# Layer one's blocks 2 and 3: both h stages first, then y by seven products, with the weight work placed anew

## The chip, the core and the metric

One core of a Trainium2 chip runs one program. Its engines are TensorE (PE), VectorE (DVE), ScalarE (ACT), GpSimd (POOL) and SyncE (SP), each with a queue of its own that is worked off in program order; all DMAs of this kernel are issued on SP. The metric is the device time in microseconds of one execution.

## What is computed

Local attention over 4 batches, 8 heads, 768 tokens (chunks of 32 queries with 16 keys to the left, 8 to the right and 8 memory keys), and then two feed-forward layers on the 3072 tokens of width 512, with an inner width of 2048, all in fp32:

```python
out[:, :, c_start:c_end] = np.matmul(a, v_full)      # a: softmax over 64 keys
...
h = x @ w_in                                         # layer one
g = np.maximum(h, 0.0) + np.log1p(np.exp(-np.abs(h)))
y = g @ w_out
...
h = y @ w_in2                                        # layer two
g = h - np.tanh(h)
return (g @ w_out2).astype(np.float32)
```

## The kernel before

**Precision.** Every fp32 operand is split into a high part (a cast, on ACT) and a low part (the difference, on DVE), and each product is three matmuls (`mm3`, L385): high by high, high by low, low by high. A matmul has 128 rows of weights and 512 columns.

**Blocks.** The tokens are six blocks of 512. Layer one's block 0 runs while weights arrive, in an order written out by hand (`OPENING`). Blocks 1, 2 and 3 are plain (L925): for each of 16 slices f of the inner width PE does h(f), 12 matmuls into one of two banks `ps_h`, then y(f-2), 12 matmuls into four banks `ps_y`; ACT takes the softplus of h(f) and casts it to `gh`, DVE subtracts for `gl`. The weights of layer one stay in 16 slots of SBUF, `w0` to `w15`, but two slices that share one slot are fetched again in each block (`load_w1`).

**Blocks in pairs.** Blocks 4 and 5 of layer one, and all three pairs of blocks of layer two, use a scheme with seven products in place of eight for a 2 by 2 product of halves (`PRODUCTS`). All h of the pair come first, g stays in SBUF (`g2`), and then `y_phase` (L740) runs seven products over eight pairs of slices p: 56 steps of six matmuls. For each step `y_steps` (L695) casts the operand to `gh` on ACT and subtracts for `gl` on DVE; the operand of step s+3 is prepared right behind step s (`AHEAD` = 3), and `gh` and `gl` have three buffers each. The summed weights of this scheme are made on the chip by jobs and kept in DRAM (`wod[0]` for layer one, `wid` and `wod[1]` for layer two); `Ring` loads them in halves of 1,024 KB, each of which serves four steps, into five slots. Results of a product are copied or added in `after_y`.

**Ticks.** `tick` (L783) is called all through these stages, some 322 times, about every 12 matmuls, and hands out all other work by number: `JOBS` says at which tick each job starts. `job_w1` sums layer one's weights, `job_w` converts, sums and splits one of layer two's 16 weight pieces (it loads raw data into a single slot, waits `LEAD` = 4 ticks, then starts on ACT), and `job_x` prepares layer one's output as layer two's input.

**Attention.** Units 8 to 23 (128 tokens each) start every six ticks in `ATT_ORDER`. At the unit's tick 0 PE computes its scores into `ps_a` and the value product of the unit before; DVE takes maximum and difference; at tick 1 ACT takes one exponential of 512 columns; at tick 2 DVE sums and normalises (four instructions); at tick 4 PE transposes and ACT copies. Softplus and exponential lie in different tables of ACT, so an ACT_TABLE_LOAD stands at each change. Units 20 to 22 belong to block 5, whose x tile is still in use by block 3, so they go through DRAM (`VIA_DRAM`, `x1d`).

Of the kernel before, what the change touches and what calls it, by code (L numbers as in the profile page):

```python
# [22 lines left out]
P = 128  # L23
# [15 lines left out]
ATT_STEP = 6  # L39
ATT_ORDER = (8, 9, 10, 11, 20, 12, 13, 14, 15, 21, 16, 17, 18, 19, 22, 23)  # L40
VIA_DRAM = (20, 21, 22)
# [34 lines left out]
PLAIN = NB - 2  # L76
# [4 lines left out]
GSLOT = (8, 9, 10, 11, 12, 13, 14, 7)  # L81
JOBS = (
    (1, 15, 24, 43, 53, 76, 85, 94),
    (5, 14, 23, 33, 66, 75, 84, 92, 95, 99, 102, 106, 109, 113, 117, 152),
    (42, 54, 159, 169, 214, 224),
)
SECOND = (95, 102, 109, 117)
PHASES = ((1, NT - 1),) + tuple((2, b) for b in range(NT))
# [8 lines left out]
def attention_ffn_ffn(  # L97
# [38 lines left out]
    x1d = dpool.tile([P, KT, 2, N], F32, name="x1d")  # L136
# [230 lines left out]
    def x_out(u):  # L367
        src = att.pop(u)["x"]
        o = (u % UB) * P
        if u in VIA_DRAM:  # L370
            x = opool.tile([P, KT, 2, P], F32R, name="o")
        else:
            x = x_tile(u // UB)[:, :, :, o : o + P]
# [71 lines left out]

    def split_to(src, dst, shape):
# [12 lines left out]
    def job_w(kind, p, second=False):  # L459
# [7 lines left out]
        c = pool.tile([P, 4 * HALF], U32, name=name, bufs=1)  # L467
        nc.scalar.mul(c.bitcast(F32), hi.bitcast(F32), EXP_BIAS)
        yield
        nc.vector.tensor_scalar(out=c, in0=c, scalar1=3, scalar2=None, op0=ALU.logical_shift_left)  # L470
        for of, k, op in ((hi, 0x80000000, ALU.bitwise_and), (lo, 29, ALU.logical_shift_right)):
            nc.vector.scalar_tensor_tensor(
                out=c, in0=of, scalar=k, in1=c, op0=op, op1=ALU.bitwise_or
            )
            yield
# [10 lines left out]
        yield from split_to(w, lambda s: ((0, 4, place(s, 2, 4)),), [4, HALF])  # L486

    def sums(w):
# [3 lines left out]
        nc.vector.tensor_tensor(out=w[:, 2], in0=w[:, 2], in1=w[:, 1], op=sub)  # L492
        nc.vector.tensor_tensor(out=w[:, 3], in0=w[:, 3], in1=w[:, 1], op=sub)  # L493
# [12 lines left out]
    def job_w1(p):  # L506
        c = tpool.tile([P, 4, HALF], F32, name="c2", bufs=1)
# [10 lines left out]
    def job_x(b, e, second=False):  # L518
        raw = wpool.tile([P, 2, 2, N], F32, name="w6" if second else "w15")
# [6 lines left out]
        def high(q, src):  # L526
            if b and q in (2, 5, 7):
# [62 lines left out]
    def half_of_y(b, q, p):  # L590
        return b, "y", q, p // (NP // 2)

    uses = [
        u
        for b, (layer, _) in enumerate(PHASES)
        for u in [half_of_h(b, p, i) for p, i in h_order if layer == 2]
        + [half_of_y(b, q, p) for q in PRODUCTS for p in range(NP)]
    ]
    last_use = {u: i for i, u in enumerate(uses)}

    class Ring:
        def __init__(self, slots):
            self.todo, self.at, self.used = list(dict.fromkeys(uses)), {}, 0
            for t in slots:
                self.add(t)
# [28 lines left out]
    def kept(ps):  # L634
        t = lpool.tile([P, N], F32, name="kept", bufs=4)
# [82 lines left out]
    def after_y(b, q, d, ps):  # L718
        for _ in range(d):
            yield  # L720
        if q in (1, 6, 5):
            held[d, q] = kept(ps)
# [17 lines left out]
    def y_phase(b, prep, prepared):  # L740
        for i, q in enumerate(PRODUCTS):
            ps = [banks[(2 * b + d) % 4][i % 2] for d in range(2)]
            for p in range(NP):
# [6 lines left out]
                if p == NP // 2 and b + 1 < len(PHASES):  # L750
# [32 lines left out]
    def tick(chain=iter(())):  # L783
# [5 lines left out]
        i, r = divmod(k, ATT_STEP)  # L789
        u = ATT_ORDER[i] if i < len(ATT_ORDER) else None  # L790
        before = ATT_ORDER[i - 1] if 0 < i <= len(ATT_ORDER) else None
        if u is not None:
            if r == 1:
                if i + 2 < len(ATT_ORDER):
                    qk_load(ATT_ORDER[i + 2])
                if 0 < i < len(ATT_ORDER) - 1:
                    v_load(ATT_ORDER[i + 1])
# [3 lines left out]
        if r == 1 and before in VIA_DRAM:  # L801
            run(soft.pop(("x", before)))
# [8 lines left out]
        if r == 4 and u is not None:  # L811
            t_mm(u, ps_a[:, 0, :])
        next(chain, None)
        if r == 4 and u is not None:
# [5 lines left out]
        if r == 0 and u is not None:  # L820
            soft[u] = softmax(u)
# [5 lines left out]
    with tc.manual_schedule(engines={mybir.EngineType.PE}):  # L827
# [91 lines left out]
        def t_load(u):  # L919
            t = wpool.tile([P, 2, 2, 512], F32R, name=f"w{u % T_RING}")  # L920
# [3 lines left out]

        for j in range(1, PLAIN):  # L925
            x = x_tile(j)
            for f in range(NF):
                ps = ff_h(f, ps_h[slot % 2], x)
                tick(chain1((1, j, f), ps, nc.scalar))
                pend.append((j, f))  # L930
                run_y()
                if f == SHARED[0] + LAG:
                    defer(load_w1, SHARED[1])
                elif f == LAG - 1 and j > 1:
                    defer(load_w1, SHARED[0])
                if j == PLAIN - 1 and 0 <= f - LAG < T_RING:
                    defer(t_load, f - LAG)
                tick()
                slot += 1

        xs = [x_tile(PLAIN), None]
        steps = []
        for f in range(NF + T_LAG):
            steps += [(0, f)] * (f < NF) + [(1, f - T_LAG)] * (f >= T_LAG)
        lpool = None

        def act_g(g, ps, g0):
            softplus(g, ps)
            yield
            if g0 is not None:  # L950
                minus(g, g, g0)

        for n, (t, f) in enumerate(steps):
            ps = ps_h[(slot + n) % 2] if n < 4 else (*ps_y, *ps_h)[(n - 4) % 6]
            weights["i", f] = w1t["i", f]
            ff_h(f, ps, xs[t])
# [3 lines left out]
            if n == len(steps) - 1:  # L960
                prepared = []
                prep = y_steps(prepared)
                for _ in range(AHEAD):
                    next(prep)
            tick(act_g(g, ps, g2[f][:, 0] if t and f < NP else None))
# [3 lines left out]
            if n == 0:  # L969
                xs[1] = x_tile(PLAIN + 1)  # L970
                nc.sync.dma_start(
                    out=xs[1].bitcast(F32).rearrange("p k s n -> p (k s) n")[:, :, : P * len(VIA_DRAM)],
                    in_=x1d.rearrange("p k s n -> p (k s) n")[:, :, : P * len(VIA_DRAM)],
                )
            if now[0] > AT_END + 1 and lpool is None:
# [6 lines left out]
                ring = Ring([lpool.tile([P, 2048], F32R, name="ring")])  # L982
            if t and f % 2 and f // 2 + T_RING < NP:
                defer(t_load, f // 2 + T_RING)
            elif f == NF - 1:
                for i in (0, 2048):
                    defer(ring.add, xs[t].rearrange("p k s n -> p (k s n)")[:, i : i + 2048])
        banks = [ps_b, tuple(ps_h), tuple(ps_y[:2]), tuple(ps_y[2:])]
        for b, (layer, _) in enumerate(PHASES):
            if layer == 2:  # L990
                prepared = []
                prep = y_steps(prepared)
                h_phase(b, prep)
# [70 lines left out]
```

## Time and profile before

| what | value |
|---|---|
| median of 3 runs | 1057.54 us (1057.13 to 1058.17) |
| the profiled execution | 1057.51 us, span 1055.4 us |
| PE busy | 1044.2 us, 99% |
| DVE, ACT busy | 727.6 us (69%), 567.1 us (54%) |
| DMA | 303.19 MB, mean 287 GB/s |

The span runs from the first to the last instruction; 2.1 us of the execution's time lie outside it. PE is busy nearly all the time, so time can go where PE gets less work, and come where PE has to wait.

### The profile page before, as it was taken

To read this page: it belongs to the slowest core of one execution; us is meant where nothing else is said; L and a number is where in the kernel's file an instruction comes from. 1 tells how busy PE (TensorE), PEld (TensorE's weight loads), DVE (VectorE), ACT (ScalarE), POOL (GpSimd) and SP (SyncE) were. 2 spreads that over 40 slices of the span, in tenths; PEclk is the share of its full clock that TensorE was granted. 3 is DMA by queue.
4 is the path that set the end of the run, shared out by engine and by line. 5 is a ranking of instruction groups with operands and counts; after the bars stand their busy time and mean duration, and the time that the engine had idled before them with its cause. 6 is when DMAs were issued, how large, how long until landed. Compare 5 with 4: busy or idle time off the path is not lost.

```text
span 1055.4 us, 18458 instructions
## 1 busy us (share of the span) xinstructions
PE 1044.2 (99%) x7368; PEld 857.4 (81%) x7370; DVE 727.6 (69%) x1129; ACT 567.1 (54%) x904; POOL 7.8 (1%) x14
## 2 busy tenths in 40 slices
PE   7999999999999999999999999999999999999998
PEld 5787888888888888888888888888888888888886
DVE  6998445845755657487677687777487877446876
ACT  6996454645656455354454555544455554344553
POOL 2000000000000000000000000000000000000000
PEclk8999999999999999999999999999999999999999
DMA  9989945857777986999987999978799788656651
GB/s 377 407 327 358 337 171 186 301 187 236 263 248 248 312 307 195 341 361 352 325 326 281 359 371 347 341 294 320 272 363 347 293 321 305 224 170 213 243 202 61
DMA packets 101269, 303.19 MB, mean 287 GB/s; under 512 B 8000, under 2 KB 55104, under 8 KB 83520
## 3 DMA queue, kind: packets, MB, share of 16 engines
q1 hardware_dynamic: 101184, 302.02, 79.5%
q8 instruction: 58, 0.95, 0.4%
q14 instruction: 27, 0.22, 0.1%
HBM read 211.29 MB, written 90.70 MB: 286 GB/s over the span
## 4 chain that ended last, share of the span: by engine, by line
PE 97%; DVE 1%; ACT 1%; DMA 0%; issue 0%; ACTq 0%
PE ps_y L387 47%; PE ps_h L387 32%; PE ps_b L387 13%; PE ps_a L361 2%; PE ps_a L280 1%; PE ps_a L332 1%; PE ps_h L880 1%; DMA qk<-in_qk 0%; PE ps_yy L361 0%; PE ps_h L399 0%; DVE gl L427 0%; DVE t L307 0%; DVE x L327 0%; ACT o L170 0%; PE ps_a L268 0%
## 5 line engine op out<-in xcount | busy, mean ns | idle before, releaser
L387 PE MATMUL ps_h<-x,w 128*128 128x512 f32 x900 | 215.3, 390 | 0.1
L704 ACT CAST gh<-w 128x512 fp32r<-128x512 f32 x224 | 139.0, 622 | 140.3 <-DVE gl L645 120.2
L645 DVE TENSOR_TENSOR gl<-w,gh 128x512 fp32r<-128x512 f32 x236 | 163.0, 691 | 71.4 <-ACT gh L704 64.9
L387 PEld LDWEIGHTS ps_h<-x,w 128*128 128x128 f32 x900 | 168.6, 188 | 35.4 <-ACT t L410 0.2
L387 PE MATMUL ps_y<-gh,w 128*128 128x512 f32 x512 | 172.9, 399 | 0.0
L387 PEld LDWEIGHTS ps_y<-gh,w 128*128 128x128 f32 x512 | 96.1, 188 | 21.3
L387 PE MATMUL ps_y<-gh,x 128*128 128x512 f32 x352 | 109.4, 389 | 0.0
L387 PE MATMUL ps_y<-gl,w 128*128 128x512 f32 x256 | 99.7, 390 | 0.0
L387 PE MATMUL ps_y<-w,x 128*128 128x512 f32 x402 | 94.5, 389 | 0.0
L387 PEld LDWEIGHTS ps_y<-w,x 128*128 128x128 f32 x402 | 75.5, 188 | 15.7
L427 DVE TENSOR_TENSOR gl<-t,gh 128x512 fp32r<-128x512 f32 x64 | 45.5, 713 | 55.8 <-ACT gh L422 55.6
L668 ACT ACTIVATE tanh<-sum 128x512 f32<-128x512 f32 x72 | 45.5, 632 | 60.0 <-DVE sum L641 59.8
L387 PEld LDWEIGHTS ps_y<-gh,x 128*128 128x128 f32 x352 | 66.1, 188 | 13.7
L410 ACT ACTIVATE t<-ps_h 128x512 f32<-128x512 f32 x64 | 38.1, 598 | 69.4 <-PE ps_h L387 65.8
L387 PE MATMUL ps_b<-gh,x 128*128 128x512 f32 x176 | 68.5, 389 | 0.0
L387 PE MATMUL ps_h<-gh,x 128*128 128x512 f32 x176 | 68.5, 389 | 0.0
L387 PE MATMUL ps_y<-gl,x 128*128 128x512 f32 x176 | 68.5, 389 | 0.0
L448 ACT CAST o<-c 128x1024 fp32r<-128x1024 f32 (+1 forms) x32 | 31.0, 969 | 69.6 <-DVE c L493 41.1
L645 DVE TENSOR_TENSOR w<-w 128x512 f32<-128x512 f32 x88 | 60.5, 688 | 6.8 <-ACT w L410 5.8
L387 PEld LDWEIGHTS ps_y<-gl,w 128*128 128x128 f32 x256 | 48.2, 188 | 9.0
L387 PE MATMUL ps_y<-x,w 128*128 128x512 f32 x240 | 55.2, 389 | 0.0
L387 PE MATMUL ps_b<-w,x 128*128 128x512 f32 x216 | 54.8, 389 | 0.0
(160 smaller groups left out, 1611.6 us busy)
## 6 DMA issues: line engine op xcount, KB each, us to landing
x<-wod SPq DMA_DIRECT2D x44, 1024.0 KB, 4.7
w<-x2d SPq DMA_DIRECT2D x21, 1024.0 KB, 6.8
x<-wid SPq DMA_DIRECT2D x21, 1024.0 KB, 6.1
wod<-o SPq DMA_DIRECT2D x32, 512.0 KB, 6.1
qk<-in_qk SPq DMA_DIRECT2D x21, 768.0 KB, 6.5
x2d<-o SPq DMA_DIRECT2D x30, 512.0 KB, 7.2
x<-wid SPq DMA_DIRECT2D x18, 768.0 KB, 6.8
ring<-wod SPq DMA_DIRECT2D x12, 1024.0 KB, 5.3
```

What stands on the lines that cost most here:

```text
L280: nc.tensor.matmul(out=ps[cc, j, KEYS * p : KEYS * (p + 1)], lhsT=a["q"][r, p, cc], rhs=a["k"][r, c, p, :], start=True, stop=True,)
L332: nc.tensor.transpose(ps[:, p * P : (p + 1) * P], a["sm"][:, p * P : (p + 1) * P], ident)
L361: nc.tensor.matmul(out=ps[h : h + 64, p % 2, 2 * P + t0 : 2 * P + t0 + CHUNK], lhsT=v, rhs=pT, start=True, stop=True,)
L387: nc.tensor.matmul(out=ps, lhsT=a, rhs=b, start=first and i == 0, stop=last and i == 2, skip_group_check=on,)
L410: nc.scalar.activation(out=out, in_=x, func=AF.Softplus)
L427: eng.tensor_tensor(out=gl, in0=t, in1=gh.bitcast(F32), op=ALU.subtract)
L448: nc.scalar.copy(out=hi, in_=src)
L645: nc.vector.tensor_tensor(out=out, in0=x, in1=y, op=ALU.subtract)
L668: nc.scalar.activation(out=t, in_=h, func=AF.Tanh)
L704: nc.scalar.copy(out=gh, in_=src)
L880: nc.tensor.matmul(out=ps_h[1], lhsT=zeros[:, :P], rhs=zeros, start=True, stop=True)
```

## The change

- Blocks 2 and 3 become a pair as well: 16 h steps of block 2, 16 of block 3 in reversed order, then `y_phase(0)`, which is 56 steps. Layer one's input weights for this come back from DRAM (`T1_LOADS`), the summed output weights through a ring in slots `w0` to `w4`.
- Attention units go in plain order at ticks `ATT_AT`; the x tiles are free by then, and the way through DRAM is gone. Units 20 to 23 now fall into the y stage of the new pair. Units 10, 11, 21 and 22 (`LATE_ACT`) take their softmax with eight exponentials of 64 columns on ACT, which also subtract and sum.
- All `job_w1` run in block 1. Of the 16 `job_w`, seven start before tick 56, eight from tick 89 to 131 and one at 148; none starts from tick 56 to 88. Nine of them (`BY_ACT`) do more of the conversion on ACT, in three activations of 1024 columns. `split_halves` splits in halves into `gh` and `gl` buffers between ticks 105 and 121.

```diff
-ATT_STEP = 6
-ATT_ORDER = (8, 9, 10, 11, 20, 12, 13, 14, 15, 21, 16, 17, 18, 19, 22, 23)
+ATT_AT = (0, 6, 14, 20, 28, 33, 38, 42, 46, 50, 54, 59, 64, 68, 74, 86, 92)
...
+    (8, 15, 27, 37, 43, 49, 55, 89, 96, 99, 102, 105, 108, 111, 131, 148, ),
+    (86, 94, 156, 169, 206, 220, ),
...
+BY_ACT = (8, 15, 27, 55, 99, 108, 111, 131, 148, )
+T1_LOADS = {9: 0, 13: 1, 17: 2, 21: 3, 25: 4, 29: 5, 33: 6, 38: 7, 54: 0}
+LATE_ACT = (10, 11, 21, 22, )
-PHASES = ((1, NT - 1),) + tuple((2, b) for b in range(NT))
+PHASES = ((1, 1), (1, 2)) + tuple((2, b) for b in range(NT))
...
+        if by_act:
+            x = pool.tile([P, 4 * HALF, 2], U16, name=name, bufs=1)
+            nc.scalar.mul(x[:, :, 1].bitcast(F16), hi.bitcast(F32), SIGN_ONLY)
+            nc.scalar.activation(
+                out=x[:, :, 0], in_=lo, func=AF.Identity, scale=LOW_SCALE, bias=low_bias
+            )
+            nc.scalar.mul(hi.bitcast(F32), hi.bitcast(F32), EXP_BIAS)
+            yield
...
+                if not b and p % 4 == 3 and i * 2 + p // 4 >= 9:
+                    s = i * 2 + p // 4 - 9
+                    defer(t_load, s, s)
...
-            soft[u] = softmax(u)
+            soft[u] = softmax(u, u in LATE_ACT)
...
-        for j in range(1, PLAIN):
...
+        steps = [(0, f) for f in range(NF)] + [(1, f) for f in reversed(range(NF))]
+        prepared = []
+        t2 = []
+        prep = y_steps(prepared, t2)
+        ring = Ring((0,), ())
+        for n, (t, f) in enumerate(steps):
+            if t and f == NP - 1:
+                t2.extend(t2_tiles())
+            h_step(n, n == len(steps) - 1, t, f, x_tile(2 + t), t and f < NP and t2)
             if pend:
                 run_y()
                 tick()
...
+            if t and f % 2 == 0 and f < 2 * T_RING:
+                s = T1_RING[T_RING - 1 - f // 2]
+                defer(lambda s=s: ring.add(wpool.tile([P, 2048], F32R, name=f"w{s}")))
+        y_phase(0, prep, prepared)
```

How the order of instructions moves, at three places. On PE, in the middle of block 3 before (`w_...` are weight slots, x the block's input):

```order
L387 MATMUL ps_h_82<-x_2793,w_1020 128x512 x12
L387 MATMUL ps_y_670<-gh,w_890 128x512
L387 MATMUL ps_y_670<-gl,w_890 128x512
L387 MATMUL ps_y_670<-gh,w_890 128x512
L387 MATMUL ps_y_671<-gh,w_890 128x512
L387 MATMUL ps_y_671<-gl,w_890 128x512
L387 MATMUL ps_y_671<-gh,w_890 128x512
```

and on PE in the y stage of blocks 2 and 3 now, where unit 20 hands over to unit 21 (L367 is the value product, L286 the scores):

```order
L367 MATMUL ps_a<-pT,v 64x32 x32
L286 MATMUL ps_a<-qk 32x64 x32
L384 MATMUL ps_y_669<-gh,w_3701 128x512
L384 MATMUL ps_y_669<-gl,w_3701 128x512
L384 MATMUL ps_y_669<-gh,w_3701 128x512
L384 MATMUL ps_y_671<-gh,w_3701 128x512
L384 MATMUL ps_y_671<-gl,w_3701 128x512
L384 MATMUL ps_y_671<-gh,w_3701 128x512
```

A pair `gh`, `gl` served twelve matmuls and an h of another twelve stood between; now each pair serves six, with no h between, and attention stands among them.

On ACT, at one unit's scores and exponential in a plain block before (L375 copies the unit before, `o<-c` is a weight job, t and gh are block 2's softplus):

```order
L375 CAST x_3794<-ps_a 128x2x2x128
L321 ACT_TABLE_LOAD
L321 ACTIVATE sm<-sm 128x512
L448 CAST o<-c_3882 128x768
L410 ACT_TABLE_LOAD
L410 ACTIVATE t<-ps_h_82 128x512
L422 CAST gh<-t 128x512
```

and at unit 21 in the y stage of blocks 2 and 3 now (each `gh<-w` prepares one step, `t<-ps_y` is the copy of product 1):

```order
L378 CAST x_4044<-ps_a 128x2x2x128
L748 CAST gh<-w_2727 128x512
L748 CAST gh<-w_2781 128x512
L677 COPY t<-ps_y_669 128x512
L322 ACT_TABLE_LOAD
L322 ACTIVATE sm,st<-ps_a,st 128x64 x8
L748 CAST gh<-w_2802 128x512
L677 COPY t<-ps_y_671 128x512
L748 CAST gh<-w_2825 128x512
```

The table load and the eight exponentials now stand between the casts of two neighbouring steps, those of steps 10 and 11.

On ACT, at the last weight job in layer one's last y stage before:

```order
L704 CAST gh<-w_4977 128x512
L704 CAST gh<-w_5018 128x512
L704 CAST gh<-w_5061 128x512
L468 ACTIVATE c_6088<-w_5998 128x1024
L726 COPY o<-ps_h_81 128x512
```

and at the last but one in the same stage now:

```order
L748 CAST gh<-w_5568 128x512 x3
L487 ACTIVATE c_5814<-w_5718 128x1024
L488 ACTIVATE c_5814<-w_5718,low_bias 128x1024
L491 ACTIVATE w_5718<-w_5718 128x1024
L748 CAST gh<-w_5568 128x512
L748 CAST gh<-w_4869 128x512
```

The one activation stood behind the stage's last cast; now three stand in its middle, between the casts of steps 22 and 23.

## Rows read from the trace of the kernel before

**Rows 1.** The page's first part: busy us, share and instructions of each engine.

```profile
PE 1044.2 (99%) x7368; PEld 857.4 (81%) x7370; DVE 727.6 (69%) x1129; ACT 567.1 (54%) x904; POOL 7.8 (1%) x14
```

**Rows 2.** Stretches: block 1, block 3, blocks 4/5 h, blocks 4/5 y.

```profile
core 0: us, PE busy (x) PEld busy (x) DVE busy (x) ACT busy (x) POOL busy (x), PEclk, DMA share, GB/s
123.10:223.50 100.40, 100.40 (x1107) 82.38 (x1106) 58.74 (x100) 53.10 (x71) 0.00 (x0) 1.00 0.60 209
...
324.00:424.50 100.50, 100.50 (x1050) 82.68 (x1050) 62.69 (x109) 53.88 (x73) 0.00 (x0) 1.00 0.75 263
424.50:518.30 93.80, 93.80 (x474) 77.53 (x473) 62.73 (x87) 42.53 (x62) 0.00 (x0) 1.00 0.96 338
518.30:594.40 76.10, 76.10 (x337) 63.03 (x336) 55.42 (x85) 37.54 (x61) 0.00 (x0) 1.00 0.88 333
```

**Rows 3.** The chain that ended last: start us, us, what.

```profile
378.20 2.72 PE ps_y L387 x12
...
442.27 10.88 PE ps_y L387 x48
```

**Rows 4.** PE's timeline: start us, us, instruction, idle before and releaser.

```profile
105.10 0.63 PE L332 MATMUL ps_a<-ident,sm 128*128 128x128 f32 x4 [1.23 <-DVE sm L327]
...
143.76 1.14 PE L361 MATMUL ps_a<-pT,v 64*64 64x32 f32 x64
144.82 0.86 PE L280 MATMUL ps_a<-qk 64*32 64x64 f32 x64
```

**Rows 5.** ACT's timeline in layer one's last y stage.

```profile
533.43 0.62 ACT L704 CAST gh<-w 128x512 fp32r<-128x512 f32 x1 [0.74 <-DVE gl L645]
534.79 0.62 ACT L704 CAST gh<-w 128x512 fp32r<-128x512 f32 x1 [0.74 <-DVE gl L645]
```

**Rows 6.** DVE's timeline, at a unit's normalisation and in that y stage.

```profile
103.11 0.69 DVE L324 TENSOR_REDUCE st<-sm 128x8 f32<-128x512 f32 x1 [2.08 <-ACT sm L321]
...
104.27 0.69 DVE L327 TENSOR_TENSOR sm<-sm,st 128x512 f32<-128x512 f32 x1
...
534.08 0.69 DVE L645 TENSOR_TENSOR gl<-w,gh 128x512 fp32r<-128x512 f32 x1 [0.67 <-ACT gh L704]
```

**Rows 7.** ACT's timeline in the opening, at unit 5's eight exponentials.

```profile
84.33 1.28 ACT L316 ACT_TABLE_LOAD   x1
85.63 0.31 ACT L316 ACTIVATE sm<-ps_a,st 128x64 f32<-128x64 f32 x1
...
87.86 0.24 ACT L316 ACTIVATION_READ_ACCUMULATOR sm<-ps_a,st 128x1 f32 x1
```

**Rows 8.** Groups by line and shape: xcount, busy us, mean ns, idle before.

```profile
L472 DVE SCALAR_TENSOR_TENSOR c<-w,c 128x1024 uint32<-128x1024 uint32 x24 | 29.4, 1223 | 0.6
...
L468 ACT ACTIVATE c<-w 128x1024 f32<-128x1024 f32 x12 | 13.6, 1133 | 5.1 <-DVE o L452 5.1
...
L174 ACT ACTIVATE c<-w,low_bias 128x1024 uint16<-128x1024 uint32 x4 | 5.9, 1469 | 0.0
L173 ACT ACTIVATE c<-w 128x1024 f16<-128x1024 f32 x4 | 5.5, 1384 | 0.0
```

**Rows 9.** Stretches of the opening, columns as in rows 2.

```profile
15.00:20.00 5.00, 2.68 (x74) 2.12 (x75) 4.71 (x13) 5.00 (x25) 0.00 (x0) 1.00 1.03 408
20.00:25.00 5.00, 4.91 (x176) 4.58 (x178) 4.58 (x9) 4.32 (x8) 1.66 (x1) 0.58 1.03 410
...
104.00:106.00 2.00, 0.90 (x6) 0.88 (x7) 0.89 (x2) 0.23 (x1) 0.00 (x0) 1.00 1.00 355
```

**Rows 10.** DMA issues by line: xcount, KB each, median us from issue to landing.

```profile
x<-wod SPq DMA_DIRECT2D x44, 1024.0 KB, 4.7
...
w<-w1id SPq DMA_DIRECT2D x8, 1024.0 KB, 8.4
w<-in_w2o SPq DMA_DIRECT2D x8, 1024.0 KB, 8.4
```

**Rows 11.** SP's timeline: layer one's last input weights, issued in the last h stage.

```profile
479.15 0.46 SPq L921 DMA_DIRECT2D w<-w1id  x1
```

More of the change, by code (lines that the diff above doesn't have):

```diff
@@ L1 @@
+from bisect import bisect_right
 from contextlib import ExitStack
@@ L444, in out1, with split_halves @@
             defer(nc.sync.dma_start, y1d[j // 2][e % 2][:, j % 2, e // 2], o, more=1)
+    def split_halves(src, dst):
+        for s in range(2):
+            ts = []
+            for i in (0, 2):
+                t = gpool.tile([P, 2, HALF], F32R, name="gl" if s else "gh")
+                if s:
+                    nc.vector.tensor_tensor(
+                        out=t, in0=src[:, i : i + 2], in1=his[i // 2].bitcast(F32), op=ALU.subtract
+                    )
+                else:
+                    nc.scalar.copy(out=t, in_=src[:, i : i + 2])
+                ts.append(t)
+            if s:
+                for i, t in enumerate(ts):
+                    defer(put, t, ((0, 2, dst(1, 2 * i)),))
+            else:
+                his = ts
+                yield
+                for i, t in enumerate(ts):
+                    put(t, ((0, 2, dst(0, 2 * i)),))
     def split_to(src, dst, shape):
@@ L457, in put, with job_w @@
             nc.sync.dma_start(out=place, in_=t[:, at : at + n].bitcast(F32))
-    def job_w(kind, p, second=False):
+    def job_w(kind, p, second=False, by_act=False):
         src = w2i if kind == "i" else w2o
@@ L485, in job_w @@
         yield
-        yield from split_to(w, lambda s: ((0, 4, place(s, 2, 4)),), [4, HALF])
+        if T2_H[0] <= now[0] < T2_H[1]:
+            yield from split_halves(w, lambda s, i: place(s, 2 + i, 2))
+        else:
+            yield from split_to(w, lambda s: ((0, 4, place(s, 2, 4)),), [4, HALF])
     def sums(w):
@@ L591, in half_of_y, with __init__ @@
         return b, "y", q, p // (NP // 2)
[L593 to L599, printed above, removed]
-    class Ring:
-        def __init__(self, slots):
-            self.todo, self.at, self.used = list(dict.fromkeys(uses)), {}, 0
+    class Ring:
+        def __init__(self, phases, slots):
+            self.uses = [
+                u
+                for b in phases
+                for u in [half_of_h(b, p, i) for p, i in h_order if PHASES[b][0] == 2]
+                + [half_of_y(b, q, p) for q in PRODUCTS for p in range(NP)]
+            ]
+            self.last_use = {u: i for i, u in enumerate(self.uses)}
+            self.todo, self.at, self.used = list(dict.fromkeys(self.uses)), {}, 0
             for t in slots:
@@ L721, in after_y @@
         if q in (1, 6, 5):
[L722 removed]
+            held[d, q] = kept(ps, d, q)
             return
@@ L741, in y_phase @@
         for i, q in enumerate(PRODUCTS):
-            ps = [banks[(2 * b + d) % 4][i % 2] for d in range(2)]
+            ps = [(banks[2 * (b - 1) + d & 3] if b else ps_y[2 * d : 2 * d + 2])[i % 2] for d in range(2)]
             for p in range(NP):
@@ L800, in tick @@
                 run(soft.pop(u))
-        if r == 1 and before in VIA_DRAM:
-            run(soft.pop(("x", before)))
+        if k in T1_LOADS:
+            t_load(T1_LOADS[k], T1_SLOT[T1_LOADS[k]])
         active.extend(job() for job in plan.get(k, ()))
@@ L923, in t_load, with act_g @@
                 w1t["i", 2 * u + i] = t[:, i, 0], t[:, i, 1]
-        for j in range(1, PLAIN):
[L926 to L944, printed above, removed]
-        lpool = None
-        def act_g(g, ps, g0):
+        lpool = None
+        x = x_tile(1)
+        for f in range(NF):
+            ps = ff_h(f, ps_h[slot % 2], x)
+            tick(chain1((1, 1, f), ps, nc.scalar))
+            pend.append((1, f))
+            run_y()
+            if f == SHARED[0] + LAG:
+                defer(load_w1, SHARED[1])
+            tick()
+            slot += 1
+        def act_g(g, ps, g0, f=0, t2=None):
             softplus(g, ps)
@@ L959, in attention_ffn_ffn @@
             g = g2[f % NP][:, 2 * (f // NP) + t]
-            if n == len(steps) - 1:
-                prepared = []
-                prep = y_steps(prepared)
+            if last:
                 for _ in range(AHEAD):
                     next(prep)
-            tick(act_g(g, ps, g2[f][:, 0] if t and f < NP else None))
+            step()
+            tick(act_g(g, ps, g2[f][:, 0] if t and f < NP else None, f, t2))
+        steps = [(0, f) for f in range(NF)] + [(1, f) for f in reversed(range(NF))]
[7 more added lines that the diff above has]
+            h_step(n, n == len(steps) - 1, t, f, x_tile(2 + t), t and f < NP and t2)
             if pend:
@@ L968, in attention_ffn_ffn @@
                 tick()
[L969 to L975, printed above, removed]
+            if t and f % 2 == 0 and f < 2 * T_RING:
+                s = T1_RING[T_RING - 1 - f // 2]
+                defer(lambda s=s: ring.add(wpool.tile([P, 2048], F32R, name=f"w{s}")))
+        y_phase(0, prep, prepared)
+        steps = []
+        for f in range(NF + T_LAG):
+            steps += [(0, f)] * (f < NF) + [(1, f - T_LAG)] * (f >= T_LAG)
+        prepared = []
+        prep = y_steps(prepared)
+        for n, (t, f) in enumerate(steps):
+            x = x_tile(2 * (NT - 1) + t)
+            h_step(n, n == len(steps) - 1, t, f, x)
+            if now[0] > ATT_AT[-1] + 1 and lpool is None:
                 attention.close()
```

146 lines of the change are left out of this document (79 added, 67 removed).

## The prediction

> **What bounds the kernel now.** I read the page's busy times first: PE is busy 1044.2 of 1055.4 us, DVE 727.6, ACT 567.1 [rows 1]. A mean can hide stages with another limit, so the table of stretches comes next: from 123 us on PE is busy for the whole of each stage, plain or paired, at the full granted clock, while DVE and ACT have a quarter to a half of each free [rows 2]. The chain that ended last says the same: twelve matmuls take 2.72 us in a plain block and forty-eight take 10.88 us in a paired one, 0.2267 us each in both [rows 3]. The last PE wait that I found is 1.23 us at 105 us, where transposes wait for a unit's normalisation [rows 4], before the change begins. So the time is PE's work plus PE's waits, and of waits there are hardly any to remove. The question is how many the change makes.
>
> **PE's work.** Two plain blocks need 2 x 16 x 12 = 384 matmuls for y; seven products over eight pairs of slices with six matmuls each need 336. The h part stays at 384, the 16 attention units keep their matmuls. 48 fewer at 0.2267 us [rows 3] are **-10.9 us**. This term is certain as long as PE's rate holds.
>
> **How much lateness the new y stage bears.** In a plain block ACT and DVE have the time of about four groups of twelve between h(f) and y(f), some 10.9 us. In a y stage it is short. A step is six matmuls, 1.36 us. ACT's casts come every 1.36 us (533.43, 534.79), with 0.74 us of waiting in between: the trace names DVE, but the rhythm is PE's, since the cast of step s+3 needs the buffer of step s, one of three [rows 5]. The cast takes 0.62 us and the subtraction behind it 0.69 us [rows 5, 6]. With about 0.2 us for the hand-overs (the subtraction at 104.27 ends at 104.96, PE starts at 105.10 [rows 4, 6]) step s+3 is ready 1.5 us after step s ends, and PE asks for it 2.72 us after that end, when two steps are through: **1.2 us of slack**. Anything longer on ACT or DVE between two steps is a PE wait, less what attention's own matmuls give (about 1.9 us for scores and values together [rows 4]).
>
> Now the places in the two y stages where more than that stands in a row, in order:
>
> *Entry of the new y stage (unit 20).* Behind the casts of steps 0 to 2 ACT has a table load, an exponential, a table load back, the last softplus and the cast of step 3: 1.28 + 0.6 + 1.28 + 0.5 + 0.6 = 4.3 us, with the row of the table load [rows 7] and the other three as long as a cast of 512 columns [rows 5], 0.5 where the next one overlaps. Counted back from the end of the last h (scores, copy of x, three casts) they start about 1.3 us ahead of that end, so the softplus ends at +2.4 us. DVE then makes two subtractions for g and the low part of step 3, ready at +4.4 us, where PE asks at +4.1: 0.3. Behind the low part of step 4 (+5.0) DVE normalises unit 20, 1.85 us from 103.11 to 104.96 in the trace [rows 6], to +6.8; PE stands at unit 20's transposes from +5.8: 1.0. Together **+1.3 us**.
>
> *Unit 21 on ACT.* Step 7 ends product 1. ACT then has the cast of step 10 and the copy of product 1 (0.2 + 0.53 + 0.48 = 1.2 us), a table load of 1.28 us, and eight exponentials that took 85.63 to 88.10 = 2.47 us in the opening [rows 7]: 4.95 us, then the cast and subtraction of step 11: 6.4 us after step 7's end. PE asks at 3 x 1.36 = 4.1. **+2.3 us**.
>
> *Unit 22 on ACT.* The same without copy and table load: 0.73 + 2.47 + 0.62 + 0.69 + hand-over = 4.6 against 4.1. **+0.5 us**.
>
> *Unit 23* normalises without the sums that DVE has earlier, and the values of a unit stand in PE's way at its end: nothing.
>
> *The job at tick 131, in layer one's last y stage.* Before, that stage's only job, at tick 152, came to ACT behind the last cast. Now three activations of 1.38, 1.47 and 1.13 us [rows 8], with overlap 3.7 us, stand behind the cast of step 22 at 0.73: 4.4, then cast and subtraction of step 23 to 5.85, against 4.1: **+1.8 us**. Behind it DVE has one instruction of 1.22 us [rows 8], and two ticks later four in a row of about twice that; each overruns the slack by about 0.4: **+0.8 us**. The job at tick 148 again reaches ACT behind the last cast: nothing.
>
> In block 1 and in the h stages I put nothing: there ACT may be 8 to 13 us late (the two banks of h, then six), and the longest row of work I count on ACT there is 4 us plus a table load. Block 1 gets five more `job_w1` than before and one `job_w` less, about 15 us more of DVE on top of 58.7 busy of 100.4 [rows 2].
>
> At unit 21 and at the entry a rule can be held against a row. In the trace the exponential starts 0.02 us after the table load's 1.28 us end [rows 7]. The Trainium skill, page "ScalarE: Activation LUTs", section "What ACT_TABLE_LOAD costs", states that each switch also drains for some 1.38 us, 2.66 us in all; by it the two places would cost about 4 us more and the sum would be near 1057.5, no change. The row shows no drain, and I go by the row.
>
> **DMAs.** The new stages load fourteen halves of the ring and nine more times layer one's input weights, 1 MB each, and save four reloads and block 5's detour; the sizes in the program give 18 MB more in all. Where it is tight is later. In the program's sizes the last h stage of layer one issues 32.5 MB instead of 30.9 for 87.0 us of PE work, the y stage after it 29.6 instead of 26.7 for 76.2 us: 374 and 388 GB/s. The same stages ran at 338 GB/s with 0.96 of the queues busy and 333 with 0.88 [rows 2], which makes 352 to 378 at full share, taken as 365. So the queue falls behind, by 0.8 and 1.8 MB in the two stages and about 3 MB that the end of the new y stage brings, 5.6 MB or 15 us at worst. What hides it: a half of the ring is asked for 4 x 5.44 = 21.8 us ahead and lands in 4.7 us, and 17 us remain; layer one's last input weights had 18.7 us (issued at 479.15 [rows 11], first used 497.9, by 25 steps of 2.72 from 424.5 and 5.4 of the block before) for 8.4 [rows 10]. What isn't covered: the raw weights of the job at tick 131 have four ticks, 10.9 us, for a load that takes 8.4 [rows 10]. Bounds: nothing, or 8 us when it lands 10 us later. I take nothing, since ACT first has the casts to step 22 and loads of that kind arrived in time in a stage at 0.96.
>
> **Sum.** 1057.5 of the profiled execution (span 1055.4 and 2.1 outside; the median of the runs is the same) - 10.9 + 1.3 + 2.3 + 0.5 + 1.8 + 0.8 = **1053.3 us**.
>
> **Rivals.**
>
> *Hidden after all.* ACT and DVE run further ahead than I count, the waits shrink to 0 to 3 us: 1046.6 to 1050. For it: ACT and DVE sum to only 54% and 69% [rows 1], and no y stage of before shows a wait. Against: none of those stages has anything but casts and single copies on ACT.
>
> *Transfers late.* The raw load at tick 131 and the input weights of the last slices land late, 4 to 9 us more on PE: 1057.3 to 1062. It decides when the queue is over 3 us behind at tick 131, or over 10 us at the last slices. For it: 388 GB/s asked of about 365. Against: SP issues late when jobs are late, which thins the queue by itself.
>
> *The clock falls.* In the opening PE had work for 2.68 of 5 us, and the next 5 us were granted 0.58 of full speed, so partly the 1.2 GHz level; around the single wait of 1.23 us it stayed at 1.00 [rows 9]. My waits of 2.3 and 1.8 us lie between. At 0.58 five us lose 2.1 us; if the fall lasts twice that long at both waits, some 8 us are lost: 1061, slower. It decides if one wait grows to near 3 us. The Trainium skill ("TensorE: Matmul & The Clock Gate", "Part 1: The HAM clock gate") has this rule, that an idle PE is put to half rate; this trace agrees as far as the opening goes.
>
> **Chances.** A run of this kernel can tell about 0.2%, 2.1 us: faster is under 1055.4, slower over 1059.7. The forecast, 1050 to 1056.5, has 0.46 (nearly all of it faster); hidden 0.18; transfers late 0.21, half of it within 0.2%; the clock 0.09; other jams, in block 1 for one, 0.06. Faster 0.60, same 0.21, slower 0.19. The range goes from 1047 to 1061.
>
> **What would show it.** The new y stage, about 76.2 us and three units' matmuls: PE waits for DVE at steps 3 and 11 and at unit 20's transposes, 1.0 to 2.5 us each, with ACT's eight exponentials in front of step 11's cast; in the next y stage a wait behind three activations at step 23; none elsewhere; 48 matmuls fewer; the granted clock at 1.00 throughout. Wrong would be: waits on DMAs, a clock below 1.00 after 130 us, or casts that run ahead of PE by more than three steps.

## The result, and the profile after

The changed kernel takes **1068.24 us** (median of 4 runs, 1064.58 to 1070.84) where the kernel before takes 1057.34: ratio 1.0101, 95% interval 1.0070 to 1.0133. It is 11 us slower; 1053.3 was predicted.

The profiled execution took 1068.8 us with a span of 1067.0. Its page's busy times:

```profile
PE 1044.3 (98%) x7322; PEld 851.1 (80%) x7322; DVE 743.0 (70%) x1148; ACT 607.7 (57%) x1011; POOL 7.5 (1%) x14
```

The 48 matmuls are gone (7370 weight loads in [rows 1]), yet PE is as busy as before. The Trainium skill ("Perfetto Trace Analysis", "Identifying the Most-Contended Engine") states that matmul busy time is no good measure of how near PE is to its limit; here the 10.9 us of work saved do not show in it, since the matmuls that are left are drawn longer (the falls of the clock below are 5.2 us of that; the rest was not traced).

The stretches, for block 1, h of blocks 2 and 3, their y, h of blocks 4 and 5, their y (columns as in [rows 2]):

```profile
core 0: us, PE busy (x) PEld busy (x) DVE busy (x) ACT busy (x) POOL busy (x), PEclk, DMA share, GB/s
123.80:222.20 98.40, 98.40 (x977) 80.81 (x976) 67.21 (x119) 61.78 (x105) 0.00 (x0) 1.00 0.85 307
222.20:341.10 118.90, 115.39 (x1466) 93.86 (x1465) 70.31 (x110) 73.22 (x96) 0.00 (x0) 0.99 0.82 281
341.10:430.40 89.30, 87.17 (x801) 70.03 (x800) 63.65 (x108) 50.10 (x108) 0.00 (x0) 1.00 0.67 245
430.40:526.10 95.70, 91.05 (x386) 74.14 (x386) 59.38 (x86) 53.02 (x80) 0.00 (x0) 0.96 1.00 358
526.10:604.50 78.40, 77.25 (x338) 62.83 (x337) 59.09 (x91) 44.62 (x68) 0.00 (x0) 1.00 0.95 359
```

The fourth line is the worst: 384 matmuls at 0.2267 us are 87.05 us, and it lasts 95.7. PE's timeline has these waits (idle before and releaser in brackets), with the instruction that follows the one at 441.55 and the one ahead of 558.20:

```profile
243.23 0.66 PE L338 MATMUL ps_a<-ident,sm 128*128 128x128 f32 x4 [1.93 <-DVE sm L333]
340.75 0.50 PE L384 MATMUL ps_y<-x,w 128*128 128x512 f32 x1 [1.42 <-issue]
347.20 0.66 PE L338 MATMUL ps_a<-ident,sm 128*128 128x128 f32 x4 [0.49 <-DVE sm L333]
360.92 0.50 PE L384 MATMUL ps_y<-gh,w 128*128 128x512 f32 x1 [1.40 <-ACT gh L748]
361.65 0.50 PE L384 MATMUL ps_y<-gl,w 128*128 128x512 f32 x1 [0.23 <-DVE gl L686]
430.45 8.41 PE L384 MATMUL ps_h<-x,w 128*128 128x512 f32 x36
441.55 4.62 PE L384 MATMUL ps_h<-x,w 128*128 128x512 f32 x12 [2.68 <-ACT w L407]
446.00 1.32 PE L384 MATMUL ps_y<-x,w 128*128 128x512 f32 x5
502.55 7.35 PE L384 MATMUL ps_y<-x,w 128*128 128x512 f32 x24 [1.96 <-ACT w L407]
557.14 0.39 PE L384 MATMUL ps_h<-gh,ring 128*128 128x512 f32 x1
558.20 0.50 PE L384 MATMUL ps_b<-gh,ring 128*128 128x512 f32 x1 [0.67 <-ACT gh L748]
558.92 0.50 PE L384 MATMUL ps_b<-gl,ring 128*128 128x512 f32 x1 [0.23 <-DVE gl L686]
```

A wait costs more than its bracket says. From 557.14 to 558.20 are 1.06 us from start to start where 0.23 is usual: 0.83 lost, not 0.67, since the matmul before is drawn 0.39 long. Counted so, unit 21 (360.92, 361.65) costs 2.2 us and the job of tick 131 (558.20, 558.92 and one of 0.25 us later) 2.2 as well. And twelve matmuls take 4.45 us behind the wait at 441.55, not 2.72. The granted clock says why:

```profile
240.00:245.00 5.00, 3.07 (x15) 0.94 0.61 217
245.00:250.00 5.00, 5.00 (x137) 0.72 0.98 324
440.00:445.00 5.00, 3.46 (x10) 0.74 1.01 402
445.00:450.00 5.00, 5.00 (x22) 0.92 1.05 393
500.00:505.00 5.00, 3.04 (x11) 0.88 1.05 389
505.00:510.00 5.00, 5.00 (x19) 0.78 0.93 325
360.00:365.00 5.00, 3.85 (x15) 1.00 0.70 263
```

Columns: PE busy, clock, DMA share, GB/s. After each of the three waits of 1.9 us and more it falls towards the 1.2 GHz level in this execution, 1.7 us lost each time; after 1.40 us at 360.92 it stays.

**The sum.** Span +11.6 and 10.9 saved leave 22.5 us of lateness. The h stage of blocks 4 and 5 has 8.6 of it (two waits, two clock falls), 243 us has 3.7 (1.93, 1.7 and the restart), the entry of the new y stage 2.3, unit 21 2.2, the job of tick 131 2.2, the opening 0.7. Some 2.8 are left, 0.9 of them two waits at 686 us in layer two; the rest I did not trace. The 3.7 us are partly chance: runs e1, e3, e4, e5, e8 and e14 below have the same instructions up to there, and the same wait is 1.24, 0.83, 1.09, 2.35, 1.44 and 1.04 us in them. Of all seven only 1.93 and 2.35 brought the clock down.

What PE waited for, on ACT at the start of the h stage and in its middle, and on DVE at 240 us (L407 is the softplus, L570 a cast of the input job, the `job_x` of tick 86; L466 and L453 are casts of weight jobs):

```profile
433.90 1.28 ACT L407 ACT_TABLE_LOAD   x1
435.20 0.60 ACT L407 ACTIVATE w<-ps_h 128x512 f32<-128x512 f32 x1
435.69 0.61 ACT L570 CAST o<-w 128x512 fp32r<-128x512 f32 x1
440.16 0.83 ACT L466 CAST o<-w 128x768 fp32r<-128x768 f32 x1 [3.86 <-DMA y1d<-o]
440.90 1.08 ACT L407 ACTIVATE w<-ps_h 128x512 f32<-128x512 f32 x2
...
483.81 0.62 ACT L453 CAST gh<-c 128x512 fp32r<-128x512 f32 x1 [5.06 <-DMA wod<-gh]
```

```profile
240.72 0.69 DVE L438 COPY o<-ps_y 128x512 f32<-128x512 f32 x1 [4.89 <-DMA wid<-o]
```

The casts do not wait for data. They wait for a *free buffer*: `o` has four, `gh` and `gl` three each, and a buffer is free when its store to DRAM has landed (the releasers in the brackets). ACT runs in order, so the softplus at 440.90 stands behind the cast; the fourth h of the stage needs its bank. At 240.72 unit 13's normalisation stands behind DVE's copy in the same way. The stores land late (issues between 424 and 446 us; KB, median us to landing):

```profile
y1d<-o SPq DMA_DIRECT2D x2, 256.0 KB, 10.2
```

7.0 us were usual there before. But the kernel before has an even longer wait of this kind, without any PE wait:

```profile
442.72 0.83 ACT L448 CAST o<-c 128x768 fp32r<-128x768 f32 x1 [5.94 <-DMA y1d<-o]
444.50 0.59 ACT L410 ACTIVATE w<-ps_h 128x512 f32<-128x512 f32 x1
442.11 11.04 PE L387 MATMUL ps_y<-x,w 128*128 128x512 f32 x48
452.99 5.60 PE L387 MATMUL ps_h<-x,w 128*128 128x512 f32 x24
```

There the stage's first two h have a y of block 3 behind them, and the softplus held up here, at 444.50, frees a bank that PE asks for at 452.99, after four h in `ps_y`. So two things must be told apart: that ACT is late, and how much lateness the place bears.

### The profile page after: what moved, and what is told of

Read it like the earlier page. It is cut to its first block, busy times and chain, and to the rows that moved or that the text cites. A ratio compares the mean times of both kernels' runs of the same rounds, so it can differ in the third digit from the quotient of the medians.

```text
span 1067.0 us, 18604 instructions
## 1 busy us (share of the span) xinstructions
PE 1044.3 (98%) x7322; PEld 851.1 (80%) x7322; DVE 743.0 (70%) x1148; ACT 607.7 (57%) x1011; POOL 7.5 (1%) x14
## 4 chain that ended last, share of the span: by engine, by line
PE 83%; DVE 6%; DMA 5%; ACT 4%; issue 2%; SPq 0%; ACTq 0%; DVEq 0%
PE ps_y L384 44%; PE ps_h L384 22%; PE ps_b L384 12%; PE ps_a L367 2%; DMA wod<-gl 2%; PE ps_a L286 1%; DMA ring<-wod 1%; DVE w L686 1%; DVE gl L686 1%; DMA wod<-o 1%; PE ps_a L338 1%; DMA wid<-o 1%; ACT gh L748 1%; DMA x2d<-o 0%; PE ps_h L928 0%
## 5 line engine op out<-in xcount | busy, mean ns | idle before, releaser
L748 ACT CAST gh<-w 128x512 fp32r<-128x512 f32 x280 | 173.5, 624 | 170.1 <-DVE gl L686 126.6
L686 DVE TENSOR_TENSOR gl<-w,gh 128x512 fp32r<-128x512 f32 x298 | 204.7, 690 | 93.6 <-ACT gh L748 86.6
L384 PE MATMUL ps_h<-x,w 128*128 128x512 f32 x660 | 159.6, 394 | 2.8 <-ACT w L407 2.7
L384 PE MATMUL ps_y<-gh,w 128*128 128x512 f32 x480 | 157.8, 396 | 1.4 <-ACT gh L748 1.4
L384 PEld LDWEIGHTS ps_h<-x,w 128*128 128x128 f32 x660 | 124.0, 189 | 29.7 <-ACT w L407 3.3
L384 PE MATMUL ps_y<-x,w 128*128 128x512 f32 x480 | 116.6, 400 | 3.4 <-ACT w L407 2.0
L384 PEld LDWEIGHTS ps_y<-x,w 128*128 128x128 f32 x480 | 91.7, 193 | 23.8 <-ACT w L407 2.4
L384 PEld LDWEIGHTS ps_y<-w,x 128*128 128x128 f32 x402 | 75.5, 188 | 15.7
L686 DVE TENSOR_TENSOR w<-w 128x512 f32<-128x512 f32 x104 | 71.6, 688 | 16.3 <-ACT w L407 15.0
L682 DVE TENSOR_TENSOR sum<-ps_y,kept 128x512 f32<-128x512 f32 x36 | 24.9, 691 | 43.4 <-PE ps_y L384 37.0
L686 DVE TENSOR_TENSOR w<-w,w 128x512 f32<-128x512 f32 x80 | 54.9, 686 | 0.0
```

The source lines that it names most:

```text
L384: nc.tensor.matmul(out=ps, lhsT=a, rhs=b, start=first and i == 0, stop=last and i == 2, skip_group_check=on,)
L682: nc.vector.tensor_tensor(out=h, in0=ps, in1=t, op=ALU.add)
L686: nc.vector.tensor_tensor(out=out, in0=x, in1=y, op=ALU.subtract)
L748: nc.scalar.copy(out=gh, in_=src)
```

## The experiments

**Theory A**: stores under way hold the shared buffers, in the stages that I put at nothing. **B**: the rows of work in the y stages, as predicted, only longer. **C**: the jobs' own work on ACT and DVE. **D**: a full queue, late loads. All runs are edits of the changed kernel; the kernel before gave 1057.3 to 1058.4 beside them.

**1. Take B's places away.**

```diff
-LATE_ACT = (10, 11, 21, 22, )
+LATE_ACT = (10, 11)
-    (..., 108, 111, 131, 148, ),
+    (..., 108, 111, 148, 152, ),
```

> Units 21 and 22 get one exponential each instead of eight on ACT, and the job of tick 131 goes back to tick 152. Theory A (buffers held by stores that have not landed, in the stages that the prediction put at nothing): only the waits at 361 and 558 to 568 us can go, 2.8 us; the waits near 243, 441 and 502 us and the three falls of the granted clock stay; 1065 to 1068 us. Rival B (the rows of work on ACT and DVE inside the y stages, as the prediction priced them, carry the loss): 1055 to 1060.

Measured: 1075.21 us, ratio 1.0166 (1.0145 to 1.0187). The wait at 361 us shrinks to 0.52, the ones at 558 and after are gone, those at 441 and 502 stay (3.05, 2.58): B is real at its two places and falls as the cause of the loss. A's number is missed too: two jobs four ticks apart make new waits of 4.96, 3.16 and 1.26 us at the start of layer two, where a cast of the first waits 3.35 us for `y1d<-o` again.

**2. Move the weight job of tick 27**, to 33 with its neighbours (e2) or to 23 alone (e6).

```diff
-    (8, 15, 27, 37, 43, 49, 55, 89, 96, 99, 102, 105, 108, 111, 131, 148, ),
+    (8, 15, 33, 39, 45, 50, 55, 89, 96, 99, 102, 105, 108, 111, 131, 148, ),
```

> The weight job of tick 27 moves to 33 (its neighbours by one or two ticks), so that its four stores are no longer under way when block 1's four outputs need the same buffers. A: the wait of 1.93 us at 243 us and the clock's fall behind it (1.75 us) go, the other two waits stay: 1068.2 - 3.7 = 1064.5. Rival C (the work of the jobs on ACT and DVE makes the lateness, not their stores): the same three activations now stand in front of softplus one stage later and a wait of 1 to 3 us moves there: 1067 to 1069. B: no change.

> The weight job of tick 27 starts at tick 23 instead, inside block 1, and nothing else moves; its stores have landed when block 1's outputs ask for buffers. A: the wait at 243 us (0.8 to 1.9 us in the runs so far) goes, and the clock's fall behind it: 1068.2 - 1 to 3.7 = 1064.5 to 1067. C: the same three activations make a wait inside block 1: 1067 to 1070.

Measured: 1068.51 (1.0099, 1.0079 to 1.0118) and 1071.04 (1.0134). The wait at 243 us is gone in both, as A says, and comes back elsewhere, as C says: 2.28 us at 333 (ACT behind DVE's work for the jobs of 50 and 55), or 3.77 us at 225 (unit 12's output waits on DVE, which then has the weight jobs of 22, 23, 25 and 28). Both theories hold, each in its place; in e6 DVE had also waited 4.35 us for a buffer (`wid<-o`) until 208 us, so that place is not C's alone. Neither run is faster than the changed kernel.

**3. More buffers in the h stage, nothing else** (idle tiles of the next stage; the second kernel also for the first half of the job of tick 89).

```diff
-    t = gpool.tile([P, 2, HALF], F32R, name="gl" if s else "gh")
+    if i:
+        t = lpool.tile([P, N], F32R, name="sum" if s else "kept", bufs=3 if s else 4)
+    else:
+        t = gpool.tile([P, 2, HALF], F32R, name="gl" if s else "gh")
```

> The second halves of the jobs at ticks 102 to 111 use seven buffers that lie idle until the next stage, besides the six that they had; every operation, store and load stays. A: the wait of 1.96 us at 502 us and the clock's fall behind it go (3.7 us), those at 243 and 441 stay: 1064.5. C and rival D (a full DMA queue makes loads late): no change, 1067 to 1069.

> As the kernel with more buffers for ticks 102 to 111, and the first half of the job of tick 89 in two pieces from the same idle buffers, so that its cast no longer stands on ACT behind the outputs' stores in front of the third softplus. A: the waits at 441 us (2.68) and 502 us (1.96) go with their two clock falls (1.75 each): 1068.2 - 8.1 = 1060. C and D: 1066 to 1069.

Measured: 1065.38 (1.0090, 1.0059 to 1.0122) and 1063.81 (1.0063, 1.0040 to 1.0085). In the second (e4) the wait at 441 us is gone: A holds there. The one near 500 us stays in both (1.89 and 2.85, and 1.28 more at 508 in e4): the 5 us for `wod<-gh` are gone, and ACT waits for the next late things, in e3 a raw load, which is D, in e4 already at 448 us the input job's own buffers. The stage itself (table at the end of this section) is not shorter in e3, and 3.5 us shorter in e4:

```profile
494.04 1.37 ACT L491 ACTIVATE w<-w 128x1024 f16<-128x1024 f32 x1 [4.31 <-DMA w<-in_w2o]
```

```profile
448.44 0.62 ACT L590 CAST o<-w 128x512 fp32r<-128x512 f32 x1 [6.75 <-DMA x2d<-o]
```

So these buffers alone are not the cause there. I widened A: the queue is full in that stage, and whatever ACT wants of it comes late. The two jobs that make layer two's input bring 4.5 MB each of the stage's 34.

**4. Move both input jobs out of the h stage**, to ticks 66 and 78 in the y stage (e5; e7 with the other edits), then to 62 and 72, between that stage's outputs (e8; e9 with the other edits).

```diff
-    (86, 94, 156, 169, 206, 220, ),
+    (66, 78, 156, 169, 206, 220, ),
-X_SLOT = (15, 7, 15, 15, 15, 15, )
+X_SLOT = (15, 15, 15, 15, 15, 15, )
-            if q in (2, 5, 7):
+            if b and q in (2, 5, 7):
```

> The two jobs that turn layer one's outputs into layer two's inputs (each reads 1 MB and stores 3.5 MB) start at ticks 66 and 78, inside the new y stage, instead of 86 and 94; all their results go through the shared buffers, none through gh and gl. Theory A in its wider form (the DMA queue is full in the h stage of blocks 4 and 5, so that whatever ACT needs from it, a buffer whose store has landed or a raw load, comes late, and softplus stands behind it): that stage loses 9 MB, its waits at 441 and 502 us (2.68 and 1.96) and their two clock falls (1.75 each) go: 1060; up to 2 us come back as waits for DVE inside the y stage. Rival C (the weight jobs' own work on ACT and DVE): both waits stay, 1067 to 1070.

> Together: the two input jobs in the y stage, the weight job at tick 23, the job of tick 131 at tick 114 in the h stage, which has room again, and units 21 and 22 with one exponential each. A: 1068.2 - 8.1 - 2 - 1.15 - 1.2 = 1055.5, faster than the kernel before by 2 us; C and B: above 1062.

> As the kernel with the two input jobs in the y stage, but at ticks 62 and 72, so that their seven stores each fall between the y stage's own outputs (ticks 72, 84, 88, 92) and not on them. Wide form of A, in which the waits at 380 and 422 us of that kernel are again outputs that ask for buffers held by x2d stores under way: those waits (2.4 and 3.5 us with two clock falls) go, and the h stage of blocks 4 and 5 stays free of waits: 1068.2 - 8.1 = 1060, with up to 2 us more where unit 20 and 21 meet the first job's casts. If the y stage cannot bear seven casts and eleven subtractions of a job at all (rival C for this stage), 2 to 6 us of waits stay wherever the jobs stand: 1064 to 1068.

> The input jobs at ticks 62 and 72, the weight job of tick 27 at 32 (the next one at 38), the job of tick 131 at 114, units 21 and 22 with one exponential each. If every cause is named rightly only the entry (1.9 us) and small waits are left of 11.4 and none of the clock falls: 1068.2 - 8.1 - 2 to 3.7 - 1.15 - 1.2 = 1054 to 1056, faster than before. If the waits only move to another place: 1060 to 1068.

Measured: 1070.04 (1.0116), 1070.77 (1.0125), 1064.85 (1.0081), 1060.42 (1.0040, 1.0022 to 1.0058). In all four the h stage has no wait. At 66 and 78 the y stage pays it back and is 10.6 to 12.6 us longer, with waits of 2.4 to 3.9 us (neighbouring ones added) where its own outputs want buffers that hold input stores; DVE in e7, which has both jobs there too:

```profile
378.40 0.69 DVE L773 TENSOR_TENSOR o<-ps_y,t 128x512 f32<-128x512 f32 x1 [1.91 <-DMA x2d<-o]
```

Between the outputs (62, 72) these go; but 3.47 us at the entry come in e8, and 1.75 us at 363 in e9. Waits moved in all four: my sums, which only subtracted, were 4 to 15 us too low.

**5. One input job at 72, the other left at 94**, with 27 to 32, 37 to 38 and one exponential for units 21 and 22; e10 also 131 to 114, e12 also 49 and 55 to 48 and 53. The moved job's casts for products 2, 5 and 7 go through `o` in place of `gh` and `gl`.

```diff
-    (86, 94, 156, 169, 206, 220, ),
+    (72, 94, 156, 169, 206, 220, ),
-            if q in (2, 5, 7):
+            if (b or e) and q in (2, 5, 7):
```

> One input job at tick 72 in the y stage and the other at 94 in the h stage behind it; tick 32 for the early weight job, the last but one weight job at tick 114, one exponential for units 21 and 22. The h stage of blocks 4 and 5 then moves 32 MB again, as in the kernel before, which had no wait there. If the first input job at tick 62 made the waits of 1.75 us at 363 us and 0.4 at 375: 1060.4 - 2.2 = 1058. If a full queue alone makes that stage's waits (wide A), one of 2 to 3 us comes back there with a clock fall: 1062.

> The same with the weight job at tick 131 in the next y stage, as in the changed kernel, so that the h stage moves 2.75 MB less, about 29 MB for 87 us or 337 GB/s: by A no wait is left there, 1.15 us stay at the job of tick 131: 1058 + 1.15 = 1059; by C (rows of work, not transfers) both variants show the same waits in the h stage.

> The last mix (input jobs at 72 and 94, weight job at 131) with the weight jobs of ticks 49 and 55 at 48 and 53, so that the last one's subtraction of 1.22 us is no longer among the instructions that DVE has in front of the y stage's first low parts. If that lateness of DVE makes the wait of 1.41 us at the entry, it goes, and the 0.5 us at unit 20's transposes shrink: 1057.1 - 1.5 to 2 = 1055.3, faster than the kernel before by 2 us. If the table loads and the exponential on ACT make it (the step as predicted): no change, 1057.

Measured: 1058.42 (1.0007, 0.9994 to 1.0021), 1057.08 (0.9997, 0.9988 to 1.0006), 1056.47 (1.0005, 0.9992 to 1.0018): the loss is gone, a gain cannot be told. Wide A falls as it was put: the queue in e12's h stage is as full as in the changed kernel (share 1.01, there 1.00), and PE never waits.

```profile
430.00:520.00 90.00, 90.00 (x399) 74.52 (x398) 54.65 (x80) 51.52 (x78) 0.00 (x0) 1.00 1.01 372
```

e12 asked whether DVE's work for the last weight job makes the entry's wait. The wait moves, to just the two places that I had worked out, 0.3 at step 3 and 1.0 at unit 20's transposes, but it does not shrink: from unit 20's scores to its transposes PE takes 11.45 us in the changed kernel, 11.36 in e12 and 11.37 in e1, e3, e5, e6, e7 and e14 (e8 and e10 are longer). First the changed kernel, then e12:

```profile
335.75 0.86 PE L286 MATMUL ps_a<-qk 64*32 64x64 f32 x64
338.81 1.28 ACT L327 ACT_TABLE_LOAD   x1
342.67 1.42 DVE L686 TENSOR_TENSOR w<-w 128x512 f32<-128x512 f32 x2 [0.88 <-ACT w L407]
...
332.74 0.86 PE L286 MATMUL ps_a<-qk 64*32 64x64 f32 x64
341.74 0.50 PE L384 MATMUL ps_y<-gl,w 128*128 128x512 f32 x1 [0.40 <-DVE gl L686]
344.10 0.66 PE L338 MATMUL ps_a<-ident,sm 128*128 128x128 f32 x4 [0.94 <-DVE sm L333]
```

In both kernels DVE waits there for ACT's softplus (0.88 us, in e12 1.60), which stands behind two table loads and the exponential: the result is that expectation's second branch, the step as predicted.

**6. The one move alone, and a denser stage.** e14 is the changed kernel with 86 to 72 and that job's casts through `o`, as in the fence above, and no other edit; e13 is e12 with eight weight jobs in the h stage (89, 94, 97, 100, 103, 106, 109, 112).

> The changed kernel with one edit: the first input job at tick 72, in the y stage, instead of 86; the second stays at 94, all weight jobs stay. Narrow A: with that job's stores gone from the start of the h stage the waits at 441 and 502 us and their clock falls go, 8.1 us, and at most 1 us comes back in the y stage; the wait near 243 us stays: 1060 to 1061. Wide A: the wait at 502 us, in the middle of the stage, stays (1.96 and 1.75): 1064.

> The best mix so far with the weight job of tick 131 brought into the h stage: jobs at 89, 94, 97, 100, 103, 106, 109, 112 (the last not by ACT) for 89, 96, 99, 102, 105, 108, 111, 131. Narrow A (what counts is that stores under way hold buffers when the first softpluses of a stage stand behind them): no wait in the h stage, and the 1.2 us behind the job of tick 131 go with their restarts: 1056.5 - 2 = 1054.5. Wide A (a full queue, about 32 MB in shorter time, makes ACT late as such): waits of 2 to 3 us come back in the h stage: 1058 to 1061.

Measured: e14 **1058.50** (1.0006, 0.9997 to 1.0016), 9.7 us less than the changed kernel and less than either form of A expected. Of the 10.0 us between the two profiled spans 8.6 lie in the h stage. Another 2.5 lie at 243 us, ahead of the move, where the wait happened to be 1.04 us and the clock stayed; and the y stage, with the job in it, is 1.4 us longer. So the move is worth some 7 us, by one profiled execution of each, and the rest is mostly chance.

e13 1064.99 (1.0070, 1.0049 to 1.0091): waits of 3.73 and 1.68 us return in the h stage, which wide A expected and narrow A excluded, at a time above both. Yet the queue ahead of the first wait is less full than e12's (share 0.93 against 1.03 from 430 to 475 us), and ACT's casts wait for stores there:

```profile
472.70 0.83 ACT L466 CAST o<-c 128x768 fp32r<-128x768 f32 x1 [3.54 <-DMA x2d<-o]
474.08 5.49 PE L384 MATMUL ps_h<-x,w 128*128 128x512 f32 x12 [3.73 <-ACT w L407]
```

So neither form of A holds as it was put. What fits all runs, and is argued more than shown, is a request for a buffer that a store still holds, against the slack of its place. In e14 ACT waits nearly as long as in the changed kernel, the first time 14.4 us into the stage and not 9.7, behind banks that bear it:

```profile
437.70 0.60 ACT L407 ACTIVATE w<-ps_h 128x512 f32<-128x512 f32 x1 [2.12 <-PE ps_h L384]
440.42 0.60 ACT L407 ACTIVATE w<-ps_h 128x512 f32<-128x512 f32 x1 [1.19 <-PE ps_h L384]
443.73 0.62 ACT L570 CAST o<-w 128x512 fp32r<-128x512 f32 x1 [2.72 <-DMA wid<-o]
...
474.47 0.62 ACT L453 CAST gh<-c 128x512 fp32r<-128x512 f32 x1 [5.67 <-DMA wod<-gh]
492.38 0.59 ACT L407 ACTIVATE w<-ps_y 128x512 f32<-128x512 f32 x1
```

Its first four softpluses wait for PE, not PE for them, and the six banks carry the 5.67 us. The softplus that PE missed by 1.96 us at 502.55 is done at 492.97 here, and PE asks for that bank 24 steps of 2.72 after the stage's start at 429.34, at 494.6.

Lengths on PE in us, start to start: the new y stage from unit 20's transposes to the next stage's first h, and that h stage to its first y product.

| run | y stage of blocks 2 and 3 | h stage of blocks 4 and 5 |
|---|---|---|
| changed kernel | 83.2 | 95.6 |
| e3 | 83.2 | 96.5 |
| e4 | 84.7 | 92.2 |
| e5, e7 | 95.8, 93.8 | 87.0, 87.0 |
| e8, e9 | 89.0, 87.1 | 87.0, 87.0 |
| e12 | 82.7 | 87.0 |
| e13 | 82.7 | 95.7 |
| e14 | 84.6 | 87.1 |

## Why the prediction was wrong

- **The step that failed**: "In block 1 and in the h stages I put nothing: there ACT may be 8 to 13 us late". For the first four h of a stage that was wrong. A plain block has a y between two h, so two banks bear 8 us. The new y stage leaves none over, h follows h, and a bank is asked for again 2.72 us after its own end (435.89 and 438.61 at the wait of 441.55). There the weight job of 89 asks for a buffer that the input job of 86 and the outputs hold: 3.86 us of wait on those 2.72. The kernel before has the longer ACT wait [5.94, above] at a place that bears it. At 502 us the slack was right and ACT's lateness wrong: six banks bear 13.6 us, but the softplus that PE waited for until 502.55 belongs to an h that had ended 15.7 us earlier (at 486.8, 15 steps of 2.72 from 446.00). I had counted ACT's longest row of work, 4 us, and not its waits for buffers, 3.86 and 5.06. That the input job starts this second lateness is argued from e14, where moving that job takes both PE waits away; the links between were not traced. At 243 us it is DVE that was late, 4.89 us for a buffer, where I had looked at ACT alone. Measured: 8.6 us in the h stage and 3.7 at 243, against 0.
- **DMAs, "I take nothing".** I had looked for late *loads* and for the raw load at tick 131. That one cost nothing; the *stores* did, by the buffers that they hold.
- **The clock.** I priced it and gave it 0.09, from a wait near 3 us on. It fell after 1.93, 1.96 and 2.68: 5.2 us in three falls.
- **PE's work, -10.9**: right. **Unit 21, +2.3**: right place, 2.2 from start to start. **Unit 22, +0.5**: no wait. **Job of tick 131, +2.6**: 2.2. **Entry, +1.3**: right mechanism, 1.9 idle and 2.3 from start to start; ACT's first table load (338.81) began 0.6 us ahead of the last h's end (339.4 without the wait), not 1.3. Moving DVE's last weight job (e12) changed nothing.
- **The rivals**: late transfers and the clock were both there, not in the places I named; together they passed the range's upper end.

## What to carry to other kernels

Count, for every engine that works in order, what a buffer request waits for when stores are under way, and hold it against the slack of *that* place: the first steps of a stage, with few banks and nothing between them, bear least. When a stage is replaced, the work beside its end meets a slack that is new, even if neither was touched: here one 4.5 MB job 14 ticks earlier is worth some 7 us. And a wait's price is its start-to-start excess and what the clock does after it, not the idle time in brackets.

## What was not expected of the hardware

- The clock's fall is not settled by the length of the wait. In e4 it fell to 0.66 over five us behind a wait of 1.40 us at 358.6, and stayed at 1.00 behind one of 2.85 us at 498.3 (columns as above):

```profile
360.00:365.00 5.00, 5.00 (x17) 0.66 0.69 238
500.00:505.00 5.00, 5.00 (x23) 1.00 0.95 349
```

  The Trainium skill ("TensorE: Matmul & The Clock Gate", "Part 1: The HAM clock gate") states that the point of a transition varies from run to run, since the monitor runs free of the program. These traces agree: the same wait of 1.40 us at unit 21 brings a fall in e4 and none in the changed kernel.
- In the opening, where nothing was edited, the clock falls in the profiled execution of the changed kernel and not in that of e3, which gets ten more matmuls into the same 30 us. So medians some 2 us apart say little without the stages' lengths beside them:

```profile
15.00:45.00 30.00, 28.28 (x406) 0.83 1.03 408
15.00:45.00 30.00, 26.76 (x416) 1.00 1.03 409
```

- In e9 to e13 PE stops for 1.3 to 2.0 us inside a unit's 64 scores near 274 us, 55 issued and 9 left, with no releaser in the profile. These five alone have the moves 27 to 32 and 37 to 38; what PE waits for stays open.
